# Third tile of an expert's second layer as seven block products on two column halves of TensorE

## The chip, the cores and the metric

The kernel runs on one core of a Trainium2 chip. The metric is device time in microseconds: the median of the timed runs. All arithmetic is in 32-bit floats. A core has TensorE (PE in the profile; its weight loads are PEld), VectorE (DVE), ScalarE (ACT), GpSimd (POOL) and SyncE (SP). Products are summed in PSUM, which the kernel holds as eight banks; everything else that engines work on lies in SBUF.

## The reference

Two layers one after the other. The first is a causal attention with decay, worked block by block over 768 positions for 4 batches and 8 heads of 64 channels. Its output becomes 3072 tokens of 512 channels. The second layer routes each token to one of 8 experts and is what the change touches:

```python
logits = x @ w_gate                       # (3072, 8)
expert_idx = np.argmax(logits, axis=1)
gate_w = softmax(logits)[token, expert_idx]
for e in range(E):
    xe = x[expert_idx == e]               # the expert's tokens
    h = np.maximum(xe @ w1[e], 0.0)       # 512 -> 1024, first product
    out[expert_idx == e] = gate_w * (h @ w2[e])   # 1024 -> 512, second product
```

## The kernel before

The attention fills the first 130 us. While it runs, the tokens are put on lists by expert. Then the loop at L777 takes one pass after the other. Passes 0 and 1 are expert 0's (two tiles of 128 tokens, then one and a remainder). Passes 2 to 8 are one expert each, with three tiles of 128 tokens, and passes 2, 3 and 4 have a short fourth tile of 64, 32 and 32 tokens (`LASTS`, L66). Only passes 2 to 8 use the functions with "fast" in their names, so seven passes are touched.

Strassen's form multiplies two matrices cut in 2 x 2 blocks with seven block products in place of eight, at the price of sums of blocks: `left_sums` (L497) makes s1 to s4 of the left factor, `right_sums` (L504) t1 to t4 of the right one, and `form` (L483) runs the seven products and joins them with u2 to u4. `product` issues matmuls into a PSUM bank, `give` delivers one block of the result.

A pass goes like this.

- `hidden_fast` (L542), first layer. Its left factor is the expert's w1, its right factor the tokens. It runs `form` twice, for two chunks of the hidden rows: chunk 0, then chunk 1. Each product is four matmuls, eight instructions in the profile (line L551), since each 32-bit matmul appears as two instructions. DVE joins the products (L488, L489, L492, and L560 for `give`), ACT applies the ReLU in place (L562). The products take turns in the three banks 2, 3 and 6 (L425).
- `turn` (L460) transposes the next pass's tokens on PE (L465) into banks 0 and 1; DVE and ACT copy them out (L452, L450). `token_sums` (L534) makes the next pass's right sums on DVE (L505 to L508).
- `first_sums` and `second_sums` (L521, L527) make the sums of the next expert's weights on POOL (L512, L515: eight instructions of some 2.4 us), and `fetch` gathers the tokens of the pass after (L436).
- `outputs_fast` (L572), second layer. `pair_sums` makes the left sums of the first two token tiles on DVE, each [128, 4, 128] (L498 to L501: s3, s1, s2, s4). `outputs` (L598) then does tile 2, and the short tile 3 where there is one, in the plain way: eight matmuls of 128 x 128 weights and 512 columns each (L609); the short tile puts 2 or 4 groups of partial sums side by side in the columns of the array. Last, `form` does tiles 0 and 1 together (L579; joins at L488 to L492, `give` at L590 on ACT and L591 on DVE). POOL scatters each finished tile to the output (L442).

The program order of these calls is not the order of each engine's queue. The framework lists instructions engine by engine: what it holds ready goes first, and among ready ones what comes earlier in the program. This order is fixed before the run. So `h_qsT` (L498) stands ahead of the last `give` of L560 in DVE's queue, though it is written after it.

Of the kernel before, what the change touches and what calls it, by code (L numbers as in the profile page):

```python
# [10 lines left out]
F32 = mybir.dt.float32  # L11
I32 = mybir.dt.int32
AX = mybir.AxisListType
ALU = mybir.AluOpType
ACT = mybir.ActivationFunctionType
# [5 lines left out]
def kernel(  # L21
# [29 lines left out]
    nc = tc.nc  # L51
    B, H, S, D = q.shape
    N, MD = out.shape
    E = moe_w_gate.shape[1]
    F = moe_w1.shape[2]
    P = 128
# [4 lines left out]
    FC = F // P  # L61
# [96 lines left out]
    for h in itertools.chain(range(0, H, 2), range(1, H, 2)):  # L158
        nc.vector.tensor_tensor_scan(
            out=decay[:, h % 2, h // 2, :], data0=lam_bc[:, h:h + 1].to_broadcast([P, C]),  # L160
# [11 lines left out]
    def pick(per_e, e):  # L172

        if isinstance(e, int):
            return per_e[e]
        return per_e[bass.ds(e, 1)].squeeze(0)

    def load_weights(e):
        w1t = wpool.tile([P, DC, F], F32, tag="w1", name="w1t")
        nc.sync.dma_start(out=w1t, in_=pick(w1_r, e))  # L180
        w2t = wpool.tile([P, FC, MD], F32, tag="w2", name="w2t")
        nc.sync.dma_start(out=w2t, in_=pick(w2_r, e))
        return w1t, w2t
# [4 lines left out]
    work = ctx.enter_context(tc.tile_pool(name="work", bufs=2))  # L188
    small = ctx.enter_context(tc.tile_pool(name="small", bufs=2))
    state = ctx.enter_context(tc.tile_pool(name="state", bufs=1))  # L190
    ffn = ctx.enter_context(tc.tile_pool(name="ffn", bufs=2))
# [3 lines left out]
    def bank(i, shape, name):  # L195
        return ps.tile(shape, F32, tag=f"bank{i}", name=name)
# [222 lines left out]
    def at(m, t):  # L419

        w = m.widths[t]
        return m.ids[:w, t, 0:1], m.ids[:w, t, 1:2], m.list[:w, t, 2:3]
# [3 lines left out]
    po_banks = itertools.cycle([7, 4, 5])  # L426
# [13 lines left out]
    def scatter(idx, src):  # L440

        put = nc.gpsimd.indirect_dma_start(  # L442
            out=out, out_offset=bass.IndirectOffsetOnAxis(ap=idx, axis=0), in_=src,
            in_offset=None, bounds_check=N - 1, oob_is_err=False)
        tc.declare_no_dep(put.ins, group="rows", reason="a token is on one list, once")
        tc.add_to_no_dep_group("rows", put.ins)
# [36 lines left out]
    def form(product, sums_of, temps, give):  # L483

        a, b = sums_of
        p1, u2, u3, u4 = temps
        nc.scalar.copy(p1, product(a.a11, b.b11))
        nc.vector.tensor_add(u2, product(a.s2, b.t2), p1)  # L488
        nc.vector.tensor_add(u3, product(a.s3, b.t3), u2)  # L489
        p5 = product(a.s1, b.t1)  # L490
        give(1, 1, p5, u3)
        nc.vector.tensor_add(u4, p5, u2)  # L492
        give(0, 0, product(a.a12, b.b21), p1)
        give(0, 1, product(a.s4, b.b22), u4)
        give(1, 0, product(a.a22, b.t4), u3)

    def left_sums(a, s1, s2, s3, s4, sub, add):  # L497
        sub(s3, a[0][0], a[1][0])  # L498
        add(s1, a[1][0], a[1][1])
        sub(s2, s1, a[0][0])  # L500
        sub(s4, a[0][1], s2)  # L501
        return SimpleNamespace(a11=a[0][0], a12=a[0][1], a22=a[1][1], s1=s1, s2=s2, s3=s3, s4=s4)
# [38 lines left out]

    def hidden_fast(m, w):  # L542
        m.hT = ffn.tile([P, FC, m.n], F32, tag="hT", name="hT", bufs=1)
        h = m.n // 2

        for c in range(0, FC // 2, 2):
            def product(lhs, rhs):
                p = bank(next(ph_banks), [P, 2, h], "p")
                for i in range(2):
                    for dc in range(DH):  # L550
                        nc.tensor.matmul(p[:, i, :], lhsT=lhs[:, dc, (c + i) * P:(c + i + 1) * P],  # L551
                                         rhs=rhs[:, dc, :], start=(dc == 0), stop=(dc == DH - 1))
                return p

            outs = [[m.hT[:, i * FC // 2 + c:i * FC // 2 + c + 2, k * h:(k + 1) * h]
                     for k in range(2)] for i in range(2)]
            temps = [work.tile([P, 2, h], F32, tag=t, name=f"u_{t}", bufs=n)
                     for t, n in (("qT", 2), ("kT", 2), ("qsT", 4), ("kd", 2))]
            form(product, (w, m.b), temps,
                 lambda i, k, p, u: nc.vector.tensor_add(outs[i][k], p, u))  # L560
            for i, k in ((1, 1), (0, 0), (0, 1), (1, 0)):
                nc.scalar.activation(outs[i][k], outs[i][k], ACT.Relu)  # L562

    def pair_sums(m):

        a = [[m.hT[:, j * FC // 2:(j + 1) * FC // 2, i * P:(i + 1) * P] for j in range(2)]
             for i in range(2)]
        sums = [work.tile([P, FC // 2, P], F32, tag=t, name=f"h_{t}", bufs=n)
                for t, n in (("qT", 2), ("kT", 2), ("qsT", 4), ("kd", 2))]
        return left_sums(a, *sums, nc.vector.tensor_sub, nc.vector.tensor_add)  # L570

    def outputs_fast(m, w2t, w2):  # L572
        a = pair_sums(m)
        outputs(m, w2t, range(2, len(m.widths)))

        def product(lhs, rhs):
            p = bank(next(po_banks), [P, MD // 2], "p")
            for fc in range(FC // 2):
                nc.tensor.matmul(p, lhsT=lhs[:, fc, :], rhs=rhs[:, fc, :],  # L579
                                 start=(fc == 0), stop=(fc == FC // 2 - 1))  # L580
            return p

        o = [ffn.tile([P, MD], F32, tag="o", name="o", bufs=4) for i in range(2)]
        outs = [[o[i][:, k * MD // 2:(k + 1) * MD // 2] for k in range(2)] for i in range(2)]
        two = [work.tile([P, 2, MD // 2], F32, tag="x", name="u", bufs=3) for i in range(2)]
        temps = [two[i][:, k, :] for i in range(2) for k in range(2)]

        def give(i, k, p, u):
            gate = at(m, i)[2]
            nc.scalar.activation(outs[i][k], u, ACT.Copy, scale=gate)  # L590
            nc.vector.scalar_tensor_tensor(out=outs[i][k], in0=p, scalar=gate, in1=outs[i][k],  # L591
                                           op0=ALU.mult, op1=ALU.add)

        form(product, (a, w2), temps, give)
        for i in range(2):
            scatter(at(m, i)[1], o[i])

    def outputs(m, w2t, tiles=None):  # L598
        for t in tiles or range(len(m.widths)):
            w = m.widths[t]  # L600


            k = P // w
            _, idx, gate = at(m, t)
            po = bank(next(po_banks), [P, MD], "po")

            for i, fc in enumerate((0, 1, 4, 5, 2, 3, 6, 7)):
                part = slice(i % k * w, (i % k + 1) * w)
                nc.tensor.matmul(po[part], lhsT=m.hT[:, fc, t * P:t * P + w], rhs=w2t[:, fc, :],  # L609
                                 start=(i < k), stop=(i >= FC - k), skip_group_check=True)  # L610
            o = ffn.tile([P, MD], F32, tag="o", name="o", bufs=4)
            if t % 2 or k > 1:
                nc.scalar.activation(o[:w], po[:w], ACT.Copy, scale=gate)
            else:
                nc.vector.tensor_scalar_mul(o[:w], po[:w], gate)  # L615
            for j in range(1, k):
                nc.vector.scalar_tensor_tensor(out=o[:w], in0=po[j * w:(j + 1) * w], scalar=gate,
                                               in1=o[:w], op0=ALU.mult, op1=ALU.add)
            scatter(idx, o[:w])
# [83 lines left out]
    for i in range(len(order)):  # L703
# [16 lines left out]
        if ahead:  # L720
            for s in range(2):
# [18 lines left out]
                                   op0=ALU.mult, op1=ALU.add)  # L740
# [3 lines left out]
                            in1=rkey.unsqueeze(2).to_broadcast(shp), op=ALU.is_gt)  # L744
# [6 lines left out]
    both = small.tile([P, NR, 2, NR], F32, tag="both", name="both")  # L751
# [10 lines left out]
                            op0=ALU.add, op1=ALU.max)  # L762
# [14 lines left out]
    for i, m in enumerate(passes):  # L777
        w1t, w2t = weights[max(i - 1, 0)]
        if i < 2:
            hidden(m, w1t)  # L780
        else:
            w1, w2 = w1_next, w2_next
# [23 lines left out]
    with tc.If(most > 0):  # L806
        for i in range(E):
            tiles = nc.values_load(beyond[0:1, i:i + 1], min_val=0, max_val=MORE)
            with tc.If(tiles > 0):
# [3 lines left out]
                w1t, w2t = load_weights(e)  # L813
                with tc.For_i(0, tiles, 1) as r:
                    m = SimpleNamespace(n=P, widths=[P])
# [3 lines left out]
                        out=m.list[:, 0, :], in_=pick(by_e, e)[bass.ds(r * P + CAPS[i], P), :])  # L819
# [32 lines left out]
```

## Time and profile before

| | |
|---|---|
| median of 3 runs | 478.34 us (477.48 to 478.46) |
| the profiled execution | 478.98 us |
| its span, first to last instruction | 477.2 us |
| what lies around the span | 1.78 us |
| mean granted TensorE clock | 0.997 |
| busy: PE, PEld, DVE, ACT, POOL | 96%, 80%, 47%, 27%, 52% of the span |

The parts of passes 2 to 8, from the chain of work that ended last (start of each in us; "turn and outputs" is from the first transpose to the first product of tiles 0 and 1):

| pass | hidden layer starts | turn and outputs | tiles 0 and 1 |
|---|---|---|---|
| 2 | 183.94 | 205.32 | 218.47 |
| 3 | 230.75 | 250.45 | 261.87 |
| 4 | 274.15 | 293.85 | 304.03 |
| 5 | 316.31 | 334.51 | 342.85 |
| 6 | 354.94 | 373.14 | 381.48 |
| 7 | 393.57 | 411.63 | 421.22 |
| 8 | 433.30 | 451.50 | 458.37 |

In the views of the profile, a line of the timeline holds the start, the time taken, the engine, the line of the kernel, the operation, what it writes and reads, the shape, how many instructions are merged, and in brackets the idle time before it with what ended it. A line of the chain holds start, time, engine and line. A matmul's time contains its latency, so the pace of matmuls is read from a chain's time over their number.

### The profile page before, as it was taken

What the parts mean: (1) busy time and instruction counts of PE and PEld (TensorE: products, weight loads), DVE (VectorE), ACT (ScalarE), POOL (GpSimd) and SP (SyncE); (2) the same over time, 40 slices, a digit from 0 to 9 for tenths busy, and PEclk for the clock granted to TensorE, in tenths of its full rate; (3) what the DMA queues carried; (4) which work ended last, traced back from release to release, by engine and by line L of the source; (5) the groups of instructions that cost most, each with busy time, mean ns of one, the idle gap of its engine ahead of it and who ended that gap; (6) DMA issues with size and microseconds to landing.
All of it is one profiled execution on the core that took longest, in us unless ns stands there. A gap on an engine that the chain in (4) does not pass through costs nothing.

```text
span 477.2 us, 8695 instructions
## 1 busy us (share of the span) xinstructions
PE 457.3 (96%) x3468; PEld 383.1 (80%) x3468; DVE 224.4 (47%) x525; ACT 127.0 (27%) x323; POOL 247.7 (52%) x189
## 2 busy tenths in 40 slices
PE   4799999999899999999999999999999999999994
PEld 3789999998686677957994898699699689779963
DVE  3657758585450134452345436434524623753421
ACT  3364445544320111222131122113112212211310
POOL 5423644524335829849806951991694497711001
PEclk9999999999999999999999999999999999999998
DMA  9999999999318557060506152351633615001001
GB/s 170 240 243 260 217 239 216 257 305 279 101 47 320 157 193 250 32 243 33 208 13 242 36 212 87 157 199 47 243 110 132 233 39 211 0 19 44 1 17 51
DMA packets 99856, 72.84 MB, mean 153 GB/s; under 512 B 81226, under 2 KB 81230, under 8 KB 99808
## 3 DMA queue, kind: packets, MB, share of 16 engines
q1 hardware_dynamic: 88688, 51.97, 39.2%
q0 software_dynamic: 5008, 13.41, 7.8%
q10 hardware_dynamic: 6112, 6.83, 4.3%
q8 instruction: 29, 0.48, 0.5%
q14 instruction: 19, 0.16, 0.1%
HBM read 59.13 MB, written 13.40 MB: 152 GB/s over the span
## 4 chain that ended last, share of the span: by engine, by line
PE 71%; issue 3%; DVE 1%; DMA 1%; POOL 0%; POOLq 0%; ACT 0%
PE p L551 28%; PE p L579 18%; PE po L609 16%; PE ph L475 5%; PE tp L465 3%; DMA xg<-xs,list_0a 1%; DVE h_qsT L498 0%; DVE hT L560 0%; PE tx L326 0%; POOL slots L390 0%; PE tx L328 0%; DVE xgT L452 0%; PE rank L377 0%; POOLq L805 0%; ACT hT L562 0%
## 5 line engine op out<-in xcount | busy, mean ns | idle before, releaser
L609 PE MATMUL po<-w2t,hT 128*128 128x512 f32 (+2 forms) x224 | 81.1, 597 | 0.0
L436 POOL DMA_INDIRECT xg<-xs,list x24 | 26.0, 1084 | 75.7 <-PE tp L465 70.2
L609 PEld LDWEIGHTS po<-w2t,hT 128*128 128x128 f32 (+2 forms) x224 | 31.6, 169 | 37.5 <-issue 37.2
L562 ACT ACTIVATE hT<-hT 128x384 f32<-128x384 f32 (+2 forms) x56 | 30.2, 540 | 89.8 <-DVE hT L560 89.8
L442 POOL DMA_INDIRECT out_dram<-o,list x24 | 23.7, 989 | 52.0 <-DVE o L615 28.9
L551 PE MATMUL p<-xgT,w1t 128*128 128x192 f32 (+2 forms) x224 | 42.8, 334 | 0.0
L390 POOL DMA_INDIRECT slots<-entry,slot_i x24 | 23.6, 985 | 34.9 <-DVE slot_i L388 13.7
L551 PEld LDWEIGHTS p<-xgT,w1t 128*128 128x128 f32 x224 | 38.7, 190 | 1.1 <-issue 0.8
L238 POOL TENSOR_TENSOR kd<-k_in,kdec 128x512 f32<-128x512 f32 x20 | 20.4, 1042 | 26.5 <-PE cp L301 14.7
L254 DVE TENSOR_TENSOR mt<-sp,decay 128x512 f32<-128x512 f32 x48 | 29.8, 682 | 6.2 <-PE sp L248 6.1
L591 DVE SCALAR_TENSOR_TENSOR o<-p,list,o 128x256 f32<-128x256 f32 x28 | 13.5, 483 | 32.9 <-PE p L579 17.0
L579 PE MATMUL p<-w2t,hT 128*128 128x256 f32 x112 | 26.8, 382 | 0.0
L579 PEld LDWEIGHTS p<-w2t,hT 128*128 128x128 f32 x112 | 21.0, 190 | 6.9 <-issue 4.4
L248 PE MATMUL sp<-qT,kT 64*128 64x128 f32 x384 | 24.7, 278 | 0.1
L248 PEld LDWEIGHTS sp<-qT,kT 64*128 64x128 f32 x384 | 22.4, 188 | 2.2 <-issue 1.9
L284 PE MATMUL op<-mt,v_in 128*64 128x128 f32 x384 | 23.6, 274 | 0.4 <-ACT fence L280 0.4
L475 PE MATMUL ph<-xgT,w1t 128*128 128x256 f32 (+1 forms) x128 | 23.9, 342 | 0.0
L560 DVE TENSOR_TENSOR hT<-p,u_qsT 128x384 f32<-128x384 f32 (+2 forms) x28 | 16.1, 575 | 16.5 <-PE p L551 16.5
L213 PE MATMUL tq<-ident,q_in 128*128 128x128 f32 x96 | 15.4, 286 | 7.9 <-DMA q_in<-in_q_dram 6.8
L465 PEld LDWEIGHTS tp<-ident,xg 128*128 128x128 f32 (+1 forms) x112 | 13.4, 140 | 11.7 <-issue 3.6
L293 ACT COPY xT<-op 128x512 f32<-128x512 f32 x24 | 12.9, 590 | 33.6 <-PE op L272 29.8
L488 DVE TENSOR_TENSOR u_kT<-p,u_qT 128x384 f32<-128x384 f32 (+2 forms) x14 | 8.1, 576 | 29.3 <-PE p L551 29.3
(162 smaller groups left out, 968.5 us busy)
## 6 DMA issues: line engine op xcount, KB each, us to landing
w1t<-in_moe_w_dram SPq DMA_DIRECT2D x8, 2048.0 KB, 7.7
w2t<-in_moe_w_dram SPq DMA_DIRECT2D x8, 2048.0 KB, 9.1
xs<-x ACTq DMA_DIRECT2D x24, 256.0 KB, 4.8
q_in<-in_q_dram SPq DMA_DIRECT2D x11, 512.0 KB, 8.4
k_in<-in_k_dram SPq DMA_DIRECT2D x11, 512.0 KB, 8.4
v_in<-in_v_dram SPq DMA_DIRECT2D x11, 512.0 KB, 8.7
q_in<-in_q_dram SPq DMA_DIRECT2D x2, 256.0 KB, 5.9
k_in<-in_k_dram ACTq DMA_DIRECT2D x2, 256.0 KB, 5.6
```

What stands on the lines that cost most here:

```text
L248: pin(nc.tensor.matmul(sp[u][:, i, b, :], lhsT=m.kT[s][halves[u], i, b, :], rhs=m.qT[s][halves[u], i, b, :], start=(i == 0 and b == 0), st ...
L254: nc.vector.tensor_mul(mt[:, u], sp[u], decay[:, u, s * HP // 2:(s + 1) * HP // 2].unsqueeze(2).to_broadcast(shp))
L284: pin(nc.tensor.matmul(out_at(m, b, u, hp), lhsT=m.v[:, b, 2 * hp + u, :], rhs=m.mt[hp // 2][:, u, hp % 2, b, :], start=(m.n == 0 and hp = ...
L390: put = nc.gpsimd.indirect_dma_start(out=slots, out_offset=bass.IndirectOffsetOnAxis(ap=slot_i[:, i:i + 1], axis=0), in_=entry[:, n, b, :] ...
L436: nc.gpsimd.indirect_dma_start(out=dst, out_offset=None, in_=xs[:rows, :], in_offset=bass.IndirectOffsetOnAxis(ap=idx, axis=0))
L442: put = nc.gpsimd.indirect_dma_start(out=out, out_offset=bass.IndirectOffsetOnAxis(ap=idx, axis=0), in_=src, in_offset=None, bounds_check= ...
L465: pin(nc.tensor.transpose(tp[:, t * P:t * P + w], m.xg[t // 2][:w, t % 2, dc * P:(dc + 1) * P], ident[:w, :w]))
L475: nc.tensor.matmul(ph, lhsT=w1t[:, dc, fc * P:(fc + 1) * P], rhs=m.xgT[:, dc, :], start=(dc == 0), stop=(dc == DC - 1))
L551: nc.tensor.matmul(p[:, i, :], lhsT=lhs[:, dc, (c + i) * P:(c + i + 1) * P], rhs=rhs[:, dc, :], start=(dc == 0), stop=(dc == DH - 1))
L562: nc.scalar.activation(outs[i][k], outs[i][k], ACT.Relu)
L579: nc.tensor.matmul(p, lhsT=lhs[:, fc, :], rhs=rhs[:, fc, :], start=(fc == 0), stop=(fc == FC // 2 - 1))
L609: nc.tensor.matmul(po[part], lhsT=m.hT[:, fc, t * P:t * P + w], rhs=w2t[:, fc, :], start=(i < k), stop=(i >= FC - k), skip_group_check=True)
```

## The change

Three things are changed.

1. Tile 2 of the second layer is taken out of `outputs` and done by a new `single_fast`, after tiles 0 and 1. It is cut in two halves of 64 tokens, and the seven block products have 64 weight columns each. `two` issues two products at a time: one with its result on partitions 0 to 63, the other on 64 to 127, matmuls alternating. Three calls of `two` have 256 columns; the last splits one product into two halves of 128 columns. The joins follow on DVE and ACT, on 64 partitions.
2. The left sums of the second layer are made inside `hidden_fast`, after each chunk, of that chunk's two hidden blocks: four sums for tiles 0 and 1 ([128, 2, 128]) and four for tile 2 ([128, 2, 64]), per chunk. They now stand in the program before `turn` and `token_sums`. Tile 2's sums have four new tiles in SBUF.
3. `form` runs the product a12 x b21, which needs no sums, second instead of fifth, and the ReLUs are reordered to match.

```diff
         nc.scalar.copy(p1, product(a.a11, b.b11))
+        give(0, 0, product(a.a12, b.b21), p1)
         nc.vector.tensor_add(u2, product(a.s2, b.t2), p1)
...
-        give(0, 0, product(a.a12, b.b21), p1)
         give(0, 1, product(a.s4, b.b22), u4)
...
-            for i, k in ((1, 1), (0, 0), (0, 1), (1, 0)):
+            for i, k in ((0, 0), (1, 1), (0, 1), (1, 0)):
                 nc.scalar.activation(outs[i][k], outs[i][k], ACT.Relu)
+            for a in m.sums:
+                chunks = [[block[:, c:c + 2] for block in row] for row in a.blocks]
+                left_sums(chunks, *(t[:, c:c + 2] for t in (a.s1, a.s2, a.s3, a.s4)),
+                          nc.vector.tensor_sub, nc.vector.tensor_add)
...
     def outputs_fast(m, w2t, w2):
-        a = pair_sums(m)
-        outputs(m, w2t, range(2, len(m.widths)))
+        outputs(m, w2t, range(3, len(m.widths)))
...
-        form(product, (a, w2), temps, give)
+        form(product, (m.sums[0], w2), temps, give)
         for i in range(2):
             scatter(at(m, i)[1], o[i])
+        single_fast(m, m.sums[1], w2)
...
+        def two(*products):
+            p = bank(next(po_banks), [P, half], "p2")
+            for fc in range(FC // 2):
+                for part, (lhs, rhs) in zip((lo, hi), products):
+                    nc.tensor.matmul(p[part, :rhs.shape[2]], lhsT=lhs[:, fc, :], rhs=rhs[:, fc, :],
+                                     start=(fc == 0), stop=(fc == FC // 2 - 1),
+                                     skip_group_check=True)
+            return p
...
+        p = two((a.a11, b.b11), (a.a12, b.b21))
+        nc.scalar.copy(p1, p[lo])
+        start(o[lo, :half], lo, p1)
+        add(o[lo, :half], lo, p[hi])
+        p = two((a.s2, b.t2), (a.s3, b.t3))
+        nc.vector.tensor_add(u2, p[lo], p1)
+        nc.vector.tensor_add(u3, p[hi], u2)
+        for k in range(2):
+            start(o[hi, k * half:(k + 1) * half], hi, u3)
+        p = two((a.s1, b.t1), (a.s4, b.b22))
+        nc.vector.tensor_add(u4, p[lo], u2)
+        add(o[hi, half:], hi, p[lo])
+        start(o[lo, half:], lo, u4)
+        add(o[lo, half:], lo, p[hi])
+        p = two((a.a22, b.t4[:, :, :half // 2]), (a.a22, b.t4[:, :, half // 2:]))
+        for k, part in enumerate((lo, hi)):
+            add(o[hi, k * half // 2:(k + 1) * half // 2], hi, p[part, :half // 2])
+        scatter(idx, o)
```

`start` is an ACT copy with the gate as scale (as at L590), `add` the DVE operation of L591, and `lo`, `hi` are partitions 0 to 63 and 64 to 127.

## The prediction

> **What bounds the kernel now.** I read the page first, then the chain that ended last, then the timeline of the seven fast passes engine by engine.
>
> ```profile
> PE 457.3 (96%) x3468; PEld 383.1 (80%) x3468; DVE 224.4 (47%) x525; ACT 127.0 (27%) x323; POOL 247.7 (52%) x189
> PEclk9999999999999999999999999999999999999998
> PE p L551 28%; PE p L579 18%; PE po L609 16%; PE ph L475 5%; PE tp L465 3%; DMA xg<-xs,list_0a 1%; DVE h_qsT L498 0%; DVE hT L560 0%; PE tx L326 0%; POOL slots L390 0%; PE tx L328 0%; DVE xgT L452 0%; PE rank L377 0%; POOLq L805 0%; ACT hT L562 0%
> ```
>
> PE is the bound: its three lines L551, L579 and L609 carry 62% of the span, at full clock. Only PE time, or a wait of PE, can move the result. The chain in order of time gives PE's pace in pass 8, undisturbed:
>
> ```profile
> 451.50 6.87 PE po L609 x16
> 458.37 12.10 PE p L579 x56
> ```
>
> So a 512-column instruction takes 6.87/16 = 0.429 us, a 256-column one 12.10/56 = 0.216. Tile 2 costs 6.87 us in every one of seven passes.
>
> **PE work.** The change replaces 16 instructions of 512 columns by 48 of 256 and 16 of 128, in pairs on the two halves. Do the halves run at once? The short tile of pass 2 has the same 64-column weights; its weight loads show the pace:
>
> ```profile
> 215.30 0.14 PEld L609 LDWEIGHTS po<-w2t,hT 128*64 128x64 f32 x2 [0.29 <-issue]
> 215.73 0.14 PEld L609 LDWEIGHTS po<-w2t,hT 128*64 128x64 f32 x2 [0.29 <-issue]
> 216.16 0.14 PEld L609 LDWEIGHTS po<-w2t,hT 128*64 128x64 f32 x2 [0.29 <-issue]
> ```
>
> Two loads every 0.43 us: two instructions on different halves take the time of one, 0.43 us. So 24 pairs of 256 columns cost 24 x 0.216 = 5.18 us. For 128 columns the attention has the same shape (L284): 32 instructions from 96.43 to 98.28, 0.116 us a pair, so 8 pairs are 0.93. Sum 6.11 us. Changing to half columns and back also costs: in pass 4, L609's x30 takes 7.86 us, of which 14 x 0.429 is tile 2 and 4 x 0.428 the short tile's quartets; 0.14 is left. After it the 56 instructions of L579 take 12.28 us, in pass 5, with no short tile before them, 12.09: 0.19 more. So `single_fast` is 6.11 + 0.33 = 6.44 us, 0.43 less than 6.87, and 0.62 less in pass 8, where nothing follows: 6 x 0.43 + 0.62 = **-3.2 us**. Bounds: -4.7 (no cost of changing, 128 columns at half of 0.216), 0 if the pairs lose as much as they gain.
>
> Here a page speaks against the change. The Trainium skill, "TensorE: Matmul & The Clock Gate", section "Measured speedup vs the span model", has three column tiles at 2.38 times one, an efficiency of 0.79. By that, as an estimate, 5.18 + 0.86 us become 7.6, more than 6.87, and the seven passes lose some 8 us against my sum. The row of 0.43 us a pair, in this kernel and in this form, decides against it.
>
> In passes 2 to 4 the fill between the two groups of transposes was a matmul of tile 2 (x2 of L609). Now it may be one of the short tile: a further change of 0.33 us each; I take half of three, **+0.5** (bounds 0 and 1.0).
>
> **DVE work that may be hidden.** Per chunk, four sums of 256 columns and four of 128. The rows are 0.68 us for 512 and 0.55 for 384 (L499, L506), so by their slope some 0.42 and 0.28: 2.8 us a chunk, 5.6 a pass, where four of 0.68 stood. In `single_fast`, three adds and four gated adds of the 0.42 to 0.48 us kind and two shorter ones, some 3.7 us for 0.75 (L615). DVE is busy 7.7 of 18.2 us in a hidden layer and 3.4 of 12.1 in tiles 0 and 1; PE covers this, were the sums free to run. They aren't always. Look at the end of pass 7's hidden layer, POOL and then DVE and PE:
>
> ```profile
> 410.55 2.36 POOL L515 TENSOR_TENSOR t_v<-w2t 128x1024 f32<-128x1024 f32 x1 [2.84 <-PE p L551]
> 412.86 2.80 POOL L515 TENSOR_TENSOR t_k<-w2t,t_q 128x1024 f32<-128x1024 f32 x1
> 415.74 2.54 POOL L515 TENSOR_TENSOR t_m<-w2t,t_k 128x1024 f32<-128x1024 f32 x1
> 411.65 1.80 DVE L498 TENSOR_TENSOR h_qsT<-hT 128x512 f32<-128x512 f32 x1 [0.59 <-ACT hT L562]
> 413.38 0.54 DVE L560 TENSOR_TENSOR hT<-p,u_qsT 128x384 f32<-128x384 f32 x1
> 414.49 1.59 DVE L505 TENSOR_TENSOR t_sd<-xgT 128x384 f32<-128x384 f32 x1
> 416.00 2.83 DVE L499 TENSOR_TENSOR h_qT<-hT 128x512 f32<-128x512 f32 x1
> 414.44 0.76 PE L465 MATMUL tp<-ident,xg 128*128 128x128 f32 x5 [1.05 <-DVE xgT L452]
> ```
>
> A DVE operation with both inputs in SBUF takes until POOL's running sum is over, plus its own 0.5 us: 0.68 becomes 1.8 and 2.83. One passes between two POOL instructions, no more. Those that read PSUM (L560) keep their time. PE lost 1.05 us, since the copy of the transposes (L452) stood behind the sums.
>
> So where do the new sums meet POOL? Chunk 0 ends 9.1 to 10.7 us after the hidden layer starts. In passes 3 to 6 POOL's last sum is over by then (at 235.3, 279.2, 322.0 and 361.5, chunk 0 ends at 240.6, 284.0, 325.4, 364.1), in pass 8 POOL makes none. The end of the hidden layers 3 to 6 lies 7 us ahead of POOL's next sum, behind the gathers. Those cost nothing: DVE's 2.8 us are over before PE wants the fifth product's bank, 5.2 us later. Two places are left.
>
> **Pass 2, chunk 0**, which ends at 194.63:
>
> ```profile
> 193.75 2.39 POOL L512 TENSOR_TENSOR w1t<-w1t 128x1024 f32<-128x1024 f32 x1
> 196.22 2.35 POOL L515 TENSOR_TENSOR s_q<-w1t 128x1024 f32<-128x1024 f32 x1
> 198.65 2.36 POOL L515 TENSOR_TENSOR s_v<-w1t,s_q 128x1024 f32<-128x1024 f32 x1
> ```
>
> The first sum is due at 194.4 and gets through at 196.4, the second at 199.1, the third at 201.7; five more take 1.6 us, to 203.3. Behind them in DVE's queue stands chunk 1's first `give` (the second product, done at 197.7), 0.6 us, to 203.9. It frees the bank of the fifth product, which PE could start at 194.63 + 4 x 1.52 = 200.7. PE waits **+3.0 us**. Bounds: 0, if the joins stand ahead of the sums; 4.5, if each sum that is left loses more.
>
> **Pass 7, end.** Now eight sums stand where one stood ahead of the copy L452. First sum to 413.3, last `give` and ReLU to 414.3, second sum 415.8, third 418.4, then five more and the copy. PE has transposes (0.66 us), two products of 1.73 us without sums, and then needs s2, at about 419.5, or the copy before that. It waits 3 to 5.5 us in place of 1.05; I take 4, so **+3.0 us** (bounds -1, when all fits beneath the two products, and +4.5).
>
> **End of the kernel.** After the last matmul one `give` is left now (470.50, 0.48 us). In the new order, after the third `two`, DVE has an add (0.42), two gated adds (0.48, the second behind an ACT copy of 0.5) and two of some 0.35: 2.1 us, of which the last products cover 0.93. So 1.2 us after PE instead of 0.5: **+0.7** (bounds 0 and 1.2). Tile 2's scatter comes last instead of tile 1's, at the same price.
>
> **Moved steps.** a12 x b21 second needs the ReLU of the last `give`: 1.2 us after the hidden layer, and PE has 1.73 us of a11 x b11 first. In passes 3 to 6 s2 is wanted 4.8 us after the hidden layer's end and DVE has at most 3.4 us of work ahead of it: nothing. POOL's gathers wait for the transposes, which may come later by 1.5 us, and two scatters move ahead of its weight sums; these end up to 2 us later, close to chunk 0's end in passes 6 and 7, but a single POOL sum there leaves DVE inside the 5.2 us. Nothing.
>
> **Sum.** -3.2 + 0.5 + 3.0 + 3.0 + 0.7 = +4.0 us: 478.98 + 4.0 = 483.0 against the profiled execution (span 477.2 and 1.78 around it), which lies 0.64 above the median of the runs. From the median: 478.34 + 4.0 = **482.3 us**. With the bounds of the two meetings and of PE: 476 to 489.
>
> **Rivals.**
> Faster: POOL and the sums miss each other where it matters, because the queue has chunk 1's joins and the copies ahead of the sums. Then -3.2 + 0.5 + 0.7, about 476.3; with the wait of 1.05 us gone too, 475.3. Against it: the framework lists what is ready first, and the sums are ready 3 us before the next join. The point that decides: whether DVE comes to chunk 1's first `give` in pass 2 before 200.7. Chance 0.26.
> Within 0.2% (0.96 us, about what a measurement of this kernel can tell from no change): only one of the two meetings costs PE, 478.34 - 2.0 + 3.0 = 479.3 or less. Chance 0.11.
> Lost cover: with tile 2 gone from between, the copies L452 stand behind eight sums in all passes with a `turn`, and PE's queue has the second group of transposes placed too early. If it waits 1 to 2 us in passes 2 to 6, 482.3 + 5 to 10: 490. For it: pass 7 shows that very wait. Against it: the order is listed with those durations in mind, and passes 3 to 6 show no wait now. Chance 0.12.
> The halves take turns, so the change doesn't do what it says: 48 x 0.216 + 16 x 0.108 = 12.1 for 6.87 us, some +37 in all, 519. The loads at 0.43 us a pair exclude it nearly. Chance 0.02.
> The forecast: 0.49. So faster 0.26, same 0.11, slower 0.63. The range 475.3 to 488.5 takes in the faster rival and half of the lost cover.
>
> **What would show it.** Right: `single_fast` at 6.4 us a pass; sums of chunk 0 in pass 2 of over 2 us each beside POOL's, and a PE wait at L551 of some 3 us released by L560; a wait of 3 to 5 us after pass 7's hidden layer. Wrong: no idle PE in pass 2, or waits in passes 3 to 6, or `single_fast` over 6.9 us.

## The result, and the profile after

| | before | changed |
|---|---|---|
| median, us | 478.34 (5 runs, 477.12 to 479.92) | 495.5 (5 runs, 494.44 to 500.83) |
| profiled execution, us; its span | 478.98; 477.2 | 500.83; 499.0 |

The ratio is 1.038, interval 1.034 to 1.043: slower by 17 us, where 4 were forecast and 10 were the upper end of the range. The profiled execution of the changed kernel is the longest of its five.

The page after, PE's share and clock, answers to the one before:

```profile
PE 464.2 (93%) x3804; PEld 397.7 (80%) x3804; DVE 269.0 (54%) x658; ACT 143.3 (29%) x358; POOL 246.7 (49%) x189
PEclk9999999989999999899999999799999999999997
```

PE is at 93% and the clock has notches. The rows of the view of waits that hold PE's waits in passes 2 to 8 (total us, times, longest):

```profile
PE p L589 <- DVE o L675: 8.1, 1, 8.1
PE tp L465 <- DVE xgT L452: 3.1, 2, 2.8
PE p L552 <- DVE hT L561: 2.6, 1, 2.6
```

Each is one long wait for DVE: one in pass 4, one in pass 7, one in pass 2 (the second row has another 0.3 us, ahead of pass 2). In the changed file L552 is the hidden layer, L589 tiles 0 and 1, L618 the halves, L667 the plain tiles, L675 the short tile's gated add, and L561 `give` of the hidden layer. The time from a pass's first hidden matmul to the next pass's (pass 8: to the end of the span):

| pass | before | changed | difference | before, no weight sums | changed, no weight sums |
|---|---|---|---|---|---|
| 2 | 46.7 | 51.3 | +4.6 | 46.7 | 46.9 |
| 3 | 43.4 | 43.7 | +0.3 | 43.4 | 43.7 |
| 4 | 42.2 | 52.5 | +10.4 | 42.2 | 42.7 |
| 5 | 38.6 | 38.2 | -0.4 | 38.6 | 38.2 |
| 6 | 38.6 | 38.2 | -0.4 | 38.6 | 38.2 |
| 7 | 39.7 | 42.7 | +2.9 | 38.6 | 38.4 |
| 8 | 44.0 | 45.1 | +1.0 | 44.0 | 45.3 |

The last two columns are of an experiment below. What is left of 21.8 us, 3.5, is in the attention, which the change leaves alone: one wait of 3.1 us behind a load, and slow matmuls after it. In a second profile of the same kernel this wait isn't there.

**Pass 4** is the largest loss. Timeline of DVE, POOL and PE (start, time taken):

```profile
307.34 0.74 DVE L675 SCALAR_TENSOR_TENSOR o<-po,list,o 32x512 f32<-32x512 f32 x1 [1.08 <-ACT o L671]
308.47 7.62 DVE L507 TENSOR_TENSOR t_x<-xgT,t_sd 128x384 f32<-128x384 f32 x1
308.74 2.36 POOL L515 TENSOR_TENSOR t_q<-w2t 128x1024 f32<-128x1024 f32 x1
311.05 2.34 POOL L515 TENSOR_TENSOR t_v<-w2t 128x1024 f32<-128x1024 f32 x1
313.35 2.33 POOL L515 TENSOR_TENSOR t_k<-w2t,t_q 128x1024 f32<-128x1024 f32 x1
316.13 0.74 DVE L675 SCALAR_TENSOR_TENSOR o<-po,list,o 32x512 f32<-32x512 f32 x1
316.80 1.91 DVE L508 TENSOR_TENSOR t_xT<-xgT,t_x 128x384 f32<-128x384 f32 x1
318.75 0.75 DVE L675 SCALAR_TENSOR_TENSOR o<-po,list,o 32x512 f32<-32x512 f32 x1
319.64 3.45 PE L589 MATMUL p<-t_k,h_kT 128*128 128x256 f32 x8 [8.13 <-DVE o L675]
```

DVE stands 1.08 us before the short tile's first gated add. The token sums behind it come late, and the third one, `t_x`, meets POOL's first sum of w2. It stays blocked through three POOL sums, 7.62 us for 0.55. Behind it in DVE's queue are two more gated adds of the short tile. They free the PSUM bank that PE's third product needs, so PE waits 8.13 us for work that has nothing to do with it. In the kernel before, the last token sum was over 0.85 us ahead of POOL's first:

```profile
299.13 0.55 DVE L508 TENSOR_TENSOR t_xT<-xgT,t_x 128x384 f32<-128x384 f32 x1
300.53 2.36 POOL L515 TENSOR_TENSOR t_q<-w2t 128x1024 f32<-128x1024 f32 x1
```

**After a wait**, PE is slow. Stretches of passes 2, 4 and 7 (stretch, its length, PE busy with instructions, granted clock, DMA share, GB/s):

```profile
206.82:209.97 3.15, 3.15 (x8) 0.50 0.00 0
209.97:213.20 3.23, 3.23 (x19) 0.99 0.00 0
319.64:322.93 3.29, 3.29 (x8) 0.54 0.07 16
434.19:438.90 4.71, 4.71 (x16) 0.64 0.00 0
```

Eight instructions of 224 columns take 3.15 us in place of 1.52, at half the clock. This adds 1.6 us to the 2.56 of pass 2 and 1.6 to the 8.13 of pass 4. In pass 7 it adds 1.7: the 52 instructions of L589 after the wait take 12.91 us, and 11.22 in the changed kernel without weight sums (an experiment below).

**Pass 2**, the forecast meeting (timeline of DVE, POOL and PE):

```profile
197.24 2.38 POOL L512 TENSOR_TENSOR w1t<-w1t 128x1024 f32<-128x1024 f32 x1
199.70 2.43 POOL L515 TENSOR_TENSOR s_q<-w1t 128x1024 f32<-128x1024 f32 x1
202.21 2.48 POOL L515 TENSOR_TENSOR s_v<-w1t,s_q 128x1024 f32<-128x1024 f32 x1
198.00 1.91 DVE L498 TENSOR_TENSOR h_qsT<-hT 128x256 f32<-128x256 f32 x1 [0.64 <-ACT hT L563]
200.37 1.90 DVE L498 TENSOR_TENSOR g<-hT 128x128 f32<-128x128 f32 x1
202.51 2.32 DVE L500 TENSOR_TENSOR g<-g,hT 128x128 f32<-128x128 f32 x1
206.15 0.62 DVE L561 TENSOR_TENSOR hT<-p,u_qT 128x448 f32<-128x448 f32 x1
206.82 3.34 PE L552 MATMUL p<-t_sd,w1t 128*128 128x224 f32 x8 [2.56 <-DVE hT L561]
```

Three sums get through one at a time, the join follows at 206.15 and PE after it.

**Pass 7**, the other forecast meeting (DVE and PE):

```profile
429.74 1.36 DVE L498 TENSOR_TENSOR h_qsT<-hT 128x256 f32<-128x256 f32 x1 [0.59 <-ACT hT L563]
431.49 1.97 DVE L498 TENSOR_TENSOR g<-hT 128x128 f32<-128x128 f32 x1
433.59 0.55 DVE L452 COPY xgT<-tp 128x384 f32<-128x384 f32 x1
434.19 0.66 PE L465 MATMUL tp<-ident,xg 128*128 128x128 f32 x4 [2.77 <-DVE xgT L452]
```

Two sums are held up here, and the copy of the transposes comes behind them. PE waits 2.77 us, where it waited 1.05 before.

The chain of pass 2 shows the other side, the halves at their price: 32 matmuls, x64, in 6.20 us where tile 2 took 6.87.

```profile
232.51 6.20 PE p L618 x64
```

### The profile page after: what moved, and what is told of

The parts are those of the page before. It is cut to its first block, busy times and chain, and to the rows that moved or that the text cites. A ratio compares the mean times of both kernels' runs of the same rounds, so it can differ in the third digit from the quotient of the medians.

```text
span 499.0 us, 9529 instructions
## 1 busy us (share of the span) xinstructions
PE 464.2 (93%) x3804; PEld 397.7 (80%) x3804; DVE 269.0 (54%) x658; ACT 143.3 (29%) x358; POOL 246.7 (49%) x189
## 4 chain that ended last, share of the span: by engine, by line
PE 83%; DVE 6%; DMA 5%; issue 2%; ACT 1%; SPq 1%; ACTq 0%; POOL 0%; POOLq 0%; DVEq 0%
PE p L552 26%; PE p L589 17%; PE p L618 8%; PE po L667 7%; PE ph L475 5%; PE op L284 4%; PE sp L248 4%; PE tp L465 3%; PE tx L326 2%; PE op L272 2%; DMA v_in<-in_v_dram 2%; PE cp L301 2%; PE tx L328 2%; DMA k_in<-in_k_dram 2%; DVE t_x L507 2%
## 5 line engine op out<-in xcount | busy, mean ns | idle before, releaser
L436 POOL DMA_INDIRECT xg<-xs,list x24 | 24.8, 1035 | 79.2 <-PE tp L465 73.7
L552 PE MATMUL p<-xgT,w1t 128*128 128x192 f32 (+2 forms) x224 | 41.1, 337 | 0.0
L552 PEld LDWEIGHTS p<-xgT,w1t 128*128 128x128 f32 x224 | 37.9, 190 | 1.9 <-issue 1.9
L667 PE MATMUL po<-w2t,hT 128*128 128x512 f32 (+2 forms) x112 | 33.8, 599 | 0.0
L600 ACT ACTIVATE o<-u,list 128x256 f32<-128x256 f32 x28 | 13.5, 504 | 53.5 <-DVE u L490 44.9
L284 PE MATMUL op<-mt,v_in 128*64 128x128 f32 x384 | 24.6, 280 | 3.5 <-ACT fence L280 3.5
L589 PE MATMUL p<-w2t,hT 128*128 128x256 f32 x112 | 27.8, 400 | 0.0
L589 PEld LDWEIGHTS p<-w2t,hT 128*128 128x128 f32 x112 | 21.7, 201 | 5.3 <-issue 2.5
L552 PE MATMUL p<-t_sd,w1t 128*128 128x192 f32 (+2 forms) x112 | 23.0, 351 | 2.6 <-DVE hT L561 2.6
L284 PEld LDWEIGHTS op<-mt,v_in 128*64 128x64 f32 x384 | 21.4, 140 | 4.5 <-ACT fence L280 4.2
L634 DVE SCALAR_TENSOR_TENSOR o<-p,list,o 64x256 f32<-64x256 f32 (+1 forms) x35 | 14.6, 431 | 17.1 <-ACT o L631 16.7
L667 PEld LDWEIGHTS po<-w2t,hT 128*128 128x128 f32 (+2 forms) x112 | 11.7, 147 | 15.0 <-issue 14.4
```

The costliest lines, as they stand in the source:

```text
L284: pin(nc.tensor.matmul(out_at(m, b, u, hp), lhsT=m.v[:, b, 2 * hp + u, :], rhs=m.mt[hp // 2][:, u, hp % 2, b, :], start=(m.n == 0 and hp = ...
L436: nc.gpsimd.indirect_dma_start(out=dst, out_offset=None, in_=xs[:rows, :], in_offset=bass.IndirectOffsetOnAxis(ap=idx, axis=0))
L589: nc.tensor.matmul(p, lhsT=lhs[:, fc, :], rhs=rhs[:, fc, :], start=(fc == 0), stop=(fc == FC // 2 - 1))
```

## The experiments

The theory: DVE operations with both inputs in SBUF are held up by POOL's sums of weights, and what PE needs stands behind them in DVE's queue. The rivals: the cover that tile 2 gave is lost, whatever POOL does; or the half columns are slow on PE. Ratios are against the kernel before on the same chip. The chips differ: in the first group before took 488.26 us, the surplus lying ahead of pass 2 (in this group's profiles it starts at 192 to 194 us, not 184), in the other two 477.5.

**The changed kernel again.** No edit.

> The changed kernel as it is, profiled once more. Theory (POOL's weight sums hold up DVE's sums, PE waits for the joins behind them): idle PE again in passes 2, 4 and 7, some 2.6, 8 and 3 us, each followed by matmuls at half pace, and some 495 us. The 3.5 us that the attention lost in the first profile has no cause in the change and should not come again. Rival (one bad execution): the wait of pass 4 is gone and the time is near 485.

Measured: 504.37 us beside 488.26. Waits of 2.61, 8.15 and 2.77 us in passes 2, 4 and 7; no 3.5 us in the attention. So the three waits belong to the kernel. The half clock came again after the waits of passes 4 and 7 (0.54, 0.65), but not after the 2.61 us of pass 2 (1.00). The 495 us of the expectation belong to another chip.

**No sums of weights**, on before and on the changed kernel:

```diff
...
-        return left_sums(a, a[1][0], s2, s3, s4, pool_sub, pool_add)
+        return SimpleNamespace(a11=a[0][0], a12=a[0][1], a22=a[1][1], s1=a[1][0], s2=a[0][1],
+                               s3=a[0][0], s4=a[1][1])
...
-        return right_sums(b, t1, t2, t3, t4, pool_sub_last)
+        return SimpleNamespace(b11=b[0][0], b21=b[1][0], b22=b[1][1], t1=b[0][1], t2=b[0][0],
+                               t3=b[1][1], t4=b[0][1])
```

> The kernel before without the sums of the weights on POOL: the products take raw blocks of w1 and w2 instead, so the output is not the reference's. It is the baseline for the next run. Theory: only pass 7's 1.25 us go, 477 us. Rival (POOL's sums are no hindrance to DVE): 478.3, unchanged.

> The changed kernel without the sums of the weights on POOL, raw blocks in their place (output not the reference's). Theory: no DVE sum over 0.7 us, no idle PE in passes 2, 4 and 7, and 475 to 477 us: what is left is the gain of 0.4 us a pass and a longer end. Rival 1 (lost cover: the new order of DVE and PE queues makes PE wait whatever POOL does): 488 or more. Rival 2 (the half columns are slow on PE): 490 or more with PE busy throughout.

Measured: 486.63 and 487.82 us, ratios 0.996 (0.993 to 0.998) and 1.000 (0.997 to 1.003) to before. DVE's groups in the second show no operation held up (count, busy us, mean ns):

```profile
L500 DVE TENSOR_TENSOR h_kT<-h_qT,hT 128x256 f32<-128x256 f32 x14 | 5.9, 419 | 0.0
L500 DVE TENSOR_TENSOR g<-g,hT 128x128 f32<-128x128 f32 x14 | 4.0, 287 | 0.3
L507 DVE TENSOR_TENSOR t_x<-xgT,t_sd 128x384 f32<-128x384 f32 (+2 forms) x7 | 4.0, 569 | 0.0
```

There is no wait of PE in passes 2 to 8. The change costs 1.2 us (487.82 - 486.63) without POOL's sums, and 16.1 with them on this chip (one run of the changed kernel): so some 15 us of it need POOL. Both rivals fall: in the profiles of the changed kernel with and without POOL's sums, DVE's 658 instructions and PE's 3804 stand in the same order, and without the meetings this order gives no wait. But the 0.4 us a pass that theory also expected are there in full in passes 5 and 6 only; in passes 2 to 4 the pair of columns in the table shows +0.2, +0.3 and +0.5, in pass 7 -0.2 and in pass 8 +1.3.

**Sums late.** Part 2 undone:

```diff
-            for a in m.sums:
-                chunks = [[block[:, c:c + 2] for block in row] for row in a.blocks]
...
     def outputs_fast(m, w2t, w2):
+        m.sums = hidden_blocks(m)
+        for a in m.sums:
+            left_sums(a.blocks, a.s1, a.s2, a.s3, a.s4, nc.vector.tensor_sub, nc.vector.tensor_add)
```

> The changed kernel with part 2 undone: the sums of both pairs of tiles are made whole, after the transposes and the token sums, not by chunks. Theory: pass 2's wait of 4 us is gone, pass 7's is not smaller, pass 4's goes if the token sums come ahead of POOL's first sum: 483 to 491. Rival (lost cover): PE waits for s2 in every pass, 497 or more.

Measured: 531.48 us, ratio 1.081 (1.072 to 1.090), far above what the theory expected, and as slow as the rival's open end allows. Pass 2's wait in the hidden layer is gone, as expected, but in all of passes 2 to 7 one wait of 3.1 to 6.9 us came in the second layer. Pass 6, timeline:

```profile
419.77 7.44 DVE L500 TENSOR_TENSOR g<-g,hT 128x256 f32<-128x256 f32 x1
419.98 2.36 POOL L515 TENSOR_TENSOR t_q<-w2t 128x1024 f32<-128x1024 f32 x1
422.29 2.34 POOL L515 TENSOR_TENSOR t_v<-w2t 128x1024 f32<-128x1024 f32 x1
424.59 2.33 POOL L515 TENSOR_TENSOR t_k<-w2t,t_q 128x1024 f32<-128x1024 f32 x1
```

A sum that isn't over when POOL starts on w2 loses three POOL sums again, 7.44 us for 0.42. The chunks, then, weren't the fault: made early, the sums keep clear of this place in passes 3 to 6. The rival has the waits in every pass right, but not their reason: they are for joins and gated adds, and only the 3.1 us of pass 7 are for s2.

**The order alone.** Before, with a12 x b21 second and the ReLUs reordered.

> The kernel before with part 3 alone: a12 x b21 second, ReLUs in the new order. Theory: PE is fed as before, within 0.2% of before. Rival (the new order of joins holds up the banks): 1 us or more slower.

Measured: 477.75 beside 477.46, ratio 1.000 (0.998 to 1.002), passes 2 to 7 within 0.1 us of before. Part 3 is free.

**The chunks alone.** The same, with the sums of tiles 0 and 1 by chunks; tile 2 plain:

```diff
...
+            a = m.sums
+            chunks = [[block[:, c:c + 2] for block in row] for row in a.blocks]
+            left_sums(chunks, *(t[:, c:c + 2] for t in (a.s1, a.s2, a.s3, a.s4)),
+                      nc.vector.tensor_sub, nc.vector.tensor_add)
...
```

> The kernel before with part 3 and the sums of tiles 0 and 1 by chunks; tile 2 stays plain and has no sums. Theory: four sums meet POOL in pass 2 in place of eight, so PE waits some 1 to 3 us there, half pace after it included, and pass 7 stays within 2 us of before; no wait of 8 us in pass 4, as tile 2 delays nothing: 2 to 5 us slower than before. Rival (only the half-column tile makes the trouble): within 0.5 us of before.

Measured: 478.8, ratio 1.0025 (1.0006 to 1.0043), 1.3 us slower: less than theory expected, more than the rival. Pass 2 is 48.7 us, +2.0, with a wait of 1.74 us and the clock at 1.00 after it. Passes 4 to 7 are 0.15 us shorter each. So four sums meet POOL in pass 2 too, and no long wait arises in pass 4 while tile 2 stands there.

**Weight sums in a chain.** The changed kernel, POOL's order of the sums of w2:

```diff
-        return right_sums(b, t1, t2, t3, t4, pool_sub_last)
+        pool_sub_last(t1, b[0][1], b[0][0])
+        pool_sub_last(t2, b[1][1], t1)
+        pool_sub_last(t4, b[1][0], t2)
+        pool_sub_last(t3, b[1][1], b[0][1])
```

> The changed kernel with POOL's sums of w2 in the order t1, t2, t4, t3, so that each of the first three needs the one before it. Theory A (a waiting DVE sum gets through only where POOL waits for its own last result; t1, t3, t2 run without a gap): pass 4's token sum waits for one POOL sum, 2 to 3 us in place of 7.6, and PE waits 3 to 4 us in place of 8.1. Theory B (what counts is that the DVE sum comes just as the first sum starts): 7 us again.

Measured: pass 4's wait is 3.47 us, from 8.13. Timeline of DVE and POOL:

```profile
303.96 3.04 DVE L507 TENSOR_TENSOR t_x<-xgT,t_sd 128x384 f32<-128x384 f32 x1
304.23 2.36 POOL L515 TENSOR_TENSOR t_q<-w2t 128x1024 f32<-128x1024 f32 x1
306.67 2.54 POOL L515 TENSOR_TENSOR t_k<-w2t,t_q 128x1024 f32<-128x1024 f32 x1
309.29 2.54 POOL L515 TENSOR_TENSOR t_m<-w2t,t_k 128x1024 f32<-128x1024 f32 x1
```

Same moment, same DVE operation; now the second POOL sum needs the first, starts 2.44 us after it instead of 2.31, and `t_x` passes between the two. Theory A holds here. It isn't the whole rule: in pass 7 of before, `h_qsT` passed between t_v and t_k, 2.31 us apart, which don't depend on each other; and in pass 7 of this kernel it passed between t_m (420.49) and t_v (422.80), 2.31 us apart and independent too. Time: 492.94 us in one run, the waits of passes 2 and 7 remaining (2.81, 3.73).

**The short tile moved.** The changed kernel with one line moved:

```diff
     def outputs_fast(m, w2t, w2):
-        outputs(m, w2t, range(3, len(m.widths)))
...
             scatter(at(m, i)[1], o[i])
+        outputs(m, w2t, range(3, len(m.widths)))
         single_fast(m, m.sums[1], w2)
```

> The changed kernel with one line moved: the short tile of passes 2 to 4 comes after tiles 0 and 1, ahead of the halves. Theory: in pass 4 the token sums no longer stand behind the short tile's gated adds and are over before POOL starts, so the wait of 8.1 us and the slow matmuls after it are gone; the array is changed between its modes less often, 0.5 to 1 us less in passes 2 to 4. 11 to 13 us faster than the changed kernel's median in its own comparison, 1.01 times before. The waits of passes 2 and 7 stay. Rival (POOL meets the token sums there in any order): pass 4's wait stays, 1.035 times before.

Measured: 482.19 us, ratio 1.011 (1.009 to 1.012), as expected. Pass 4 takes 41.5 us in place of 52.5; passes 2 and 7 keep waits of 2.6 and 2.8. Its DVE and POOL there:

```profile
298.69 0.55 DVE L507 TENSOR_TENSOR t_x<-xgT,t_sd 128x384 f32<-128x384 f32 x1
299.27 0.59 DVE L508 TENSOR_TENSOR t_xT<-xgT,t_x 128x384 f32<-128x384 f32 x1
300.25 2.36 POOL L515 TENSOR_TENSOR t_q<-w2t 128x1024 f32<-128x1024 f32 x1
```

The last token sum ends 0.4 us ahead of POOL's first. In the changed kernel, where the two met, the wait of 8.13 us and the half clock of 1.6 after it were the price. The rest of the 11 us comes from the short tile, which is no longer split.

**Halves where they are free.** Tile 2 in halves and the sums by chunks in passes 3 to 6 only, the short tile after the pair there; passes 2, 7 and 8 as before; own tiles for pass 7's first two sums of w2:

```diff
...
             w1, w2 = w1_next, w2_next
+            m.halves = 3 <= i <= 6
...
```

> Tile 2 in Strassen's form with sums by chunks only in passes 3 to 6, the short tile after tiles 0 and 1 there; passes 2, 7 and 8 as before; in pass 7 the first two sums of the next w2 go to tiles of their own, so that POOL can make them some 2.5 us earlier. Theory: no meeting of DVE's and POOL's sums in passes 3 to 6, 0.45 us gained in each, and pass 7's 1.25 us gone: 2 to 3.5 us faster than before. Rival (lost cover): waits in passes 3 and 4, not faster.

Measured: 475.36 us beside 477.46, ratio 0.995 (0.994 to 0.997): faster than both kernels. Passes 3 to 6 take 42.6, 41.5, 38.2 and 38.2 us. Pass 7 gained nothing (39.8): POOL's t_k still waits for PE, t_m ends at 408.9 and `h_qsT` takes 1.73 us in place of 0.68. Without a split the short tile costs 1.85 us in pass 3, in the changed kernel 1.83 + 0.99 around the transposes.

**Pass 2 as well**, its sums whole after the second chunk (`m.halves = i <= 6`, and no sums at chunk 0 there).

> As the kernel with halves in passes 3 to 6, and pass 2 as well, there with all sums whole after the second chunk, since POOL is busy at its first. Theory: the sums end before POOL's next ones start, 8 us after the hidden layer's end; pass 2 gains some 0.7 us as pass 3 did, 0.994 times before. Rival: they meet, and pass 2 loses 2 us or more.

Measured: 474.93 beside 477.47, ratio 0.9945 (0.9926 to 0.9964). Pass 2 takes 45.9 us, 0.9 less than before, with no meeting. The intervals of the two versions overlap.

## Why the prediction was wrong

The sign was right, the size wrong by 13 us. The kind of loss was foreseen: DVE's sums are held up by POOL's, and PE waits for what stands behind them. But the place where most was lost had been put at nothing, and the slow clock after a wait wasn't counted anywhere (1.6, 1.6 and 1.7 us in the profiled execution). Term by term:

- **PE work, -0.43 a pass:** right. The halves take 6.20 us and the next hidden layer 0.20 more (18.40 after 18.20), 6.40 together where 6.44 was forecast; 0.44 is gained in passes 5 and 6. The pairs run at once. The efficiency of 0.79, which the prediction worked out from the figure for three column tiles in the Trainium skill ("TensorE: Matmul & The Clock Gate", section "Measured speedup vs the span model"), isn't what two halves show here, and the measurement decides. The bound of -4.7 doesn't follow from its own terms: 24 x 0.216 + 8 x 0.108 = 6.04 us leaves 0.83 a pass, -5.8 in all.
- **The short tile split, +0.5 in all:** mis-sized. From the kernels without weight sums, passes 2 to 4 lie 0.62, 0.70 and 0.93 above the -0.43 that was due, 2.2 us together. The forecast put only one more change of mode there; the split also breaks the quartets of the short tile (1.83 + 0.99 us against 1.85).
- **Pass 2, +3.0:** the wait is 2.56 us, on the forecast path. The half clock after it, 1.6 us, wasn't counted. Of four executions with a wait of 2.56 to 2.81 us in this place it came in two: the granted clock was 0.50 in the first profile and 0.51 with the weight sums in a chain, 1.00 in the second profile and with the short tile moved.
- **Pass 7, +3.0:** +2.9 us, and this is luck. The wait is on the forecast path, but 2.77 us where 3 to 5.5 were forecast, 1.7 more than before. The half clock after it adds 1.7, and the halves give 0.4 back.
- **Pass 4, nothing:** the step that failed. The prediction asked where the new sums meet POOL, found the end of the hidden layers 3 to 6 "7 us ahead of POOL's next sum", and wrote "Those cost nothing". The new sums did get by. What met POOL was an old operation behind them, the token sum `t_x`. The prediction counted DVE's work but not DVE's own wait: the short tile's gated adds moved ahead of the token sums, and with tile 2 gone they had to wait for PE (1.08 us). Its rule "One passes between two POOL instructions, no more" failed too: three POOL sums in a row let nothing through, and `t_x` took 7.62 us for 0.55. PE waited 8.13 us, and the pass took 10.4 us more. Both halves were tested: moving the short tile removes the wait, chaining the sums reduces it to 3.47 us.
- **End, +0.7:** mis-sized. From the last matmul to the end of the span it is 8.3 us where it was 6.7: +1.6 us. DVE's part was right, since its last work ends 1.3 us after PE where it ended 0.5 after it. But the scatter isn't "at the same price": it starts 0.8 us after DVE's last work, where it started 0.3 after it, and the span ends 5.3 us after the scatter's instruction in place of 5.0. Why is open.

DVE's last work is four gated adds:

```profile
490.27 1.64 DVE L634 SCALAR_TENSOR_TENSOR o<-p,list,o 64x256 f32<-64x256 f32 x4
```

One cause stays open: why a DVE sum passes between two independent POOL sums in pass 7 (t_v and t_k, or t_m and t_v), but is held through t_q, t_v and t_k in pass 4 of the changed kernel and in passes 2 to 6 of the one with late sums, though the sums start 2.30 to 2.31 us apart in both.

## What to carry to other kernels

Before moving small operations onto an engine whose operations another can hold up, lay both queues side by side at every place. Follow the old operations that are pushed back as well as the new ones, and count the engine's own waits into when each comes: here a margin of 0.4 us lay between no wait and 8 us of it. Work that is taken off the bound engine may have been what kept the rest apart, so look at what stood behind it. Where the gain is a steady 0.4 us a pass, apply it only in those passes where nothing meets.

## What the runs showed of the hardware

- A DVE operation with two SBUF inputs can be blocked by more than the POOL instruction that runs: 7.05 to 7.8 us through three sums with no gap between them, 1.3 to 3.0 us elsewhere. The Trainium skill, "SBUF — State Buffer", section "SBUF: two separate sides", says that whichever of the two starts first holds the shared pair of ports for the whole instruction and that the other blocks fully; the short meetings agree with that for one instruction, and the long ones add that the blocked one need not be next. There the recorded starts don't bear out "first" either: `t_x` of pass 4 is recorded 0.27 us ahead of POOL's first sum (308.47 and 308.74), and it is the one that was held.
- The granted clock was 0.50 for some 3 us after PE had stood idle for 2.56 us, and stayed at 1.00 after 2.61 and 2.56 us in two other executions. The Trainium skill, "TensorE: Matmul & The Clock Gate", section "What's actually happening", has the clock halved after at least one idle window of some 3.4 us, and the window running free; 2.56 us is less than that and was enough, so the measurement decides. A free-running window would fit that the same wait is priced differently from run to run, but no run here shows the window.
- Column halves run at full overlap (a pair of 256 columns is issued every 0.21 to 0.22 us, where one instruction of 256 columns on the whole array takes 0.216), and a change between whole and half columns costs some 0.3 us there and back (6.20 us where the pairs alone were put at 6.11, and 18.40 us for the next hidden layer in place of 18.20).
